# A transformer block with adaptive layer norm: w_mod regrouped by rows, late K columns, and another order for the start of the K projection

## The chip, the cores and the metric

The kernel runs on one core of a Trainium2 chip. The metric is the device time of one execution in microseconds (us). A time quoted for a kernel is the median of several executions; the profile is of one execution, and its span (first to last instruction) is about 1.8 us shorter than that execution's time.

## The reference

Two batches (B = 2) of 256 tokens, width D = 1152 (9 tiles of 128), two heads, everything in bf16:

```python
mod = (_silu(c) @ w_mod).reshape(B, 6, 1, D)
shift_a, scale_a, gate_a, shift_m, scale_m, gate_m = [mod[:, i] for i in range(6)]
h = _layernorm(x, axis=-1) * (1 + scale_a) + shift_a
qkv = (h @ wqkv).reshape(B, N, 3, H, Dh)
...                                  # attention, wo, second layer norm, fc1, gelu, fc2
return x + gate_m * m
```

Only the start matters here: before the first real matmul, the kernel needs x, its layer norm, `scale_a` (a product of silu(c) with 1152 columns of w_mod) and the K columns of wqkv.

## The kernel before

All work is written as units, which a small list scheduler puts on the engines. TensorE (PE) and the SP queue, which issues the loads, keep the order of the source text. `mm` is one matmul (line 692), `tr` one transpose (line 695), and every `dma` has line 673; so the profile shows these three lines for nearly everything, and shapes tell them apart.

The loads in order. The weights `WSC` for `scale_a` come in two halves, columns of tiles 0 to 3 and 4 to 8 (KC = 4), each in three pieces of three k-tiles:

```python
wmod_v = w_mod.rearrange("(k p) f -> p k f", p=P)
...
dma(CSB[0:18, :], c.rearrange("b (k p) -> (b k) p", p=P), 18 * 256, "ld_c", eng="act")
for b in range(2):
    dma(X[:, 2 * b:2 * b + 2, :], xv[b], ...)
for (ka, kb) in ((0, KC), (KC, KT)):
    for k0, k1 in ((0, 3), (3, 6), (6, 9)):
        dma(WSC[:, k0:k1, ka * P:kb * P], wmod_v[:, k0:k1, D + ka * P:D + kb * P], ...)
    for kt in range(ka, kb):
        dma(WK[:, kt, :], wqkv_v[:, kt, D:2 * D], ...)
for k0 in range(0, KT, 3):
    dma(WSH[:, k0:k0 + 3, :], wmod_v[:, k0:k0 + 3, 0:D], ...)        # shift_a
```

The start of PE's program. `warm` issues matmuls on zeros that are only there to keep PE's clock up. `sca(a, b)` adds k-tiles a to b into the scale columns of tiles 0 to 3 (2-column matmuls). `xn_T(t)` transposes the normalised token tile t. `hk(kt, b)` scales a transposed tile by `1 + scale_a` into `HK`, the moving operand of the K projection:

```python
xn_T(1)
warm(1, "c")
sca(0, 3)
xn_T(0)
warm(1, "d")
sca(3, 6)
warm(2, "e")
sca(6, 9)
hk(0, 0)
sc1a(0, KC)
hk(1, 0)
... # ScalarE: copies of the other tiles, hk(2, 0), hk(3, 0)
xn_T(3, 0, 8)
xn_T(2, 0, 8)
k_first(0)                       # first-half K, batch 0, k-tile 0
xn_T(3, 8, 9)
xn_T(2, 8, 9)
k_first(1)
... # k_first(2), k_first(3), batch 1, two pairs
for kt in range(KT):
    mod_kt(WSC, kt, 0, "scb_%d" % kt, (KC, KT))     # second-half scale columns
sc1a(KC, KT)
... # hk(4..8), second-half K
```

Behind the K projection come the rows of `shift_a` ("shift rows", 2-row matmuls), their transposes, the last K tile (column tile 8, `proj(WK, 8, 17, HK, 0)`), and then Q.

Of the kernel before, what the change touches and what calls it, by code (L numbers as in the profile page):

```python
# [500 lines left out]
P = 128  # L501
# [43 lines left out]
def build_kernel(nc, x, c, wqkv, wo, w_mod, w_fc1, w_fc2, out):  # L545
# [5 lines left out]
    with (  # L551
# [81 lines left out]
        CSB = sb(misc(256), 256)  # L633
# [32 lines left out]
        wmod_v = w_mod.rearrange("(k p) f -> p k f", p=P)  # L666
# [31 lines left out]
        dma(CSB[0:18, :], c.rearrange("b (k p) -> (b k) p", p=P), 18 * 256, "ld_c", eng="act")  # L698
        for b in range(2):
            dma(X[:, 2 * b:2 * b + 2, :], xv[b], 2 * P * D * 2, "ld_x%d" % b)  # L700
        for (ka, kb) in ((0, KC), (KC, KT)):
            w = (kb - ka) * P
            for k0, k1 in ((0, 3), (3, 6), (6, 9)):
                dma(WSC[:, k0:k1, ka * P:kb * P], wmod_v[:, k0:k1, D + ka * P:D + kb * P], (k1 - k0) * P * w * 2,
                    "ld_sc%d_%d" % (ka, k0), run=w * 2)
            for kt in range(ka, kb):
                dma(WK[:, kt, :], wqkv_v[:, kt, D:2 * D], P * D * 2, "ld_wk%d" % kt, run=2304)
        for k0 in range(0, KT, 3):
            dma(WSH[:, k0:k0 + 3, :], wmod_v[:, k0:k0 + 3, 0:D], 3 * P * D * 2, "ld_sh%d" % k0, run=2304)

# [13 lines left out]
        for i in range(5):  # L724
            S.unit("pe", 430.0, "warm_a%d" % i)
            mm(ps32(5), IDENT, Q4B, True, True)
        CT_PS = ps16(6, 0, 18)
        S.unit("pe", 100, "c_T")
        tr(CT_PS, CSB[0:18, :], IDENT[0:18, 0:18])
        act(200, lambda e: e.activation(out=TH, in_=CT_PS, func=ACTF.Tanh, scale=0.5), [CT_PS], [TH], "c_tanh")  # L730
        dve(170, lambda e: e.tensor_scalar(out=HC, in0=CT_PS, scalar1=0.5, scalar2=None, op0=ALU.mult), [CT_PS], [HC], "c_half")
# [37 lines left out]
        XB = [(4, 5, 3), (6, 5, 7)]  # L769
# [32 lines left out]
        def hk(kt, b, eng="dve"):  # L802
            dst = HK[:, kt, b * 256:(b + 1) * 256]
            s1 = ps32(7, 0, 1) if kt == 0 and b == 0 else SC1A[:, kt * 2 + b:kt * 2 + b + 1]
            src = xslot(b, kt) if kt < KC else HX[:, kt, b * 256:(b + 1) * 256]
            if eng == "act":
                act(c_act(256, 1), lambda e: e.activation(out=dst, in_=src, func=ACTF.Copy, scale=s1), [src, s1], [dst], "hk_%d_%d" % (kt, b))
                return
            dve(345 if kt < KC else 285, lambda e: e.tensor_scalar(out=dst, in0=src, scalar1=s1, scalar2=None, op0=ALU.mult),
                [src, s1], [dst], "hk_%d_%d" % (kt, b))  # L810
# [7 lines left out]
        KB = [(0, 1, 2, 3), (4, 5, 6)]  # L818
# [27 lines left out]
        warm(7, "b")  # L846
# [5 lines left out]
        xn_T(0)  # L852
        warm(1, "d")
        sca(3, 6)
        warm(2, "e")
        sca(6, 9)
        hk(0, 0)
        sc1a(0, KC)
        hk(1, 0)
        xn_T_copy(0, 4, 8, "act")  # L860
        xn_T_copy(0, 8, 9, "act")
        hk(2, 0, "act")
        hk(3, 0, "act")
        xn_T(3, 0, 8)
        xn_T(2, 0, 8)

        def k_first(kt):
            for i in range(4):
                k_pair((kt,), i, 0)

        k_first(0)
        xn_T(3, 8, 9)
        xn_T(2, 8, 9)
        k_first(1)
# [9 lines left out]
        for kt in range(KT):  # L884
            mod_kt(WSC, kt, 0, "scb_%d" % kt, (KC, KT))
        sc1a(KC, KT)
        for kt in range(KC, KT):
            for b in range(2):
                hk(kt, b)
        k_pair(range(KC), 2, 1)  # L890
        for kt in range(KT):
            dma(WQ[:, kt, :], wqkv_v[:, kt, 0:D], P * D * 2, "ld_wq%d" % kt, run=2304)
            dma(WSM[:, kt, :], wmod_v[:, kt, 4 * D:5 * D], P * D * 2, "ld_sm%d" % kt, run=2304)
# [11 lines left out]

        def proj(W, j, dst_j, H, bank):
# [7 lines left out]
        k_pair(range(5), 3, 1, bank=1)  # L914
        S.unit("pe", KT * c_mm(CH) + 100.0, "shr")
        for kt in range(KT):
            for j, (f0, f1) in enumerate(sh_split):
                mm(psum[32 * j:32 * j + 2, 1024:1024 + (f1 - f0) * 128], ST[:, kt:18:9], WSH[:, kt, f0 * 128:f1 * 128],
                   kt == 0, kt == KT - 1, tile_position=(0, 32 * j))
        copy_on("dve", SHR[0:98, :], psum[0:98, 1024:1024 + CH], CH, False, "shr_ev")  # L920
        k_pair(range(5, KT), 3, 1, bank=1)
        S.unit("pe", KT * 27.0, "shT")
        for j, (f0, f1) in enumerate(sh_split):
            for f in range(f0, f1):
                mm(ps32(2, f * 2, 2), SHR[0:98, (f - f0) * 128:(f - f0 + 1) * 128], IDENT[0:98, 32 * j:32 * j + 2], f == 0, f == KT - 1,
                   skip_group_check=True)
        dma(WV, wqkv_v[:, :, 2 * D:3 * D], D * D * 2, "ld_wv", run=2304)
        for k0 in range(0, KT, 3):
            dma(WMODR[:, k0:k0 + 3, :], wmod_v[:, k0:k0 + 3, 2 * D:4 * D], 3 * P * 2 * D * 2, "ld_modr%d" % k0)
        MT1 = ps32(2, 0, 18)  # L930
        dve(170, lambda e: e.tensor_copy(SHA, MT1), [MT1], [SHA], "sha")
        for kt in range(KT):
            for b in range(2):
# [5 lines left out]
                else:  # L939
                    dve(260, lambda e, src=src, dst=dst, s2=s2: e.tensor_scalar(out=dst, in0=src, scalar1=s2, scalar2=None, op0=ALU.add),  # L940
                        [src, s2], [dst], "hx_%d_%d" % (kt, b))
        proj(WK, 8, 17, HK, 0)
# [5 lines left out]
                    "xn_1", "bn_ln1_2_1", "xn_0", "bn_ln1_2_2", "aggr_ln1_2", "var_ln1_3", "veps_ln1_2", "xn_3", "xn_2", "hk_0_0", "sc1a_0", "hk_1_0",  # L948
                    "hk_0_1", "hk_1_1", "hk_2_1", "hk_3_1", "sc1a_4"] + ["hk_%d_%d" % (kt, b) for kt in range(KC, KT) for b in range(2)],
            "act": ["ld_c", "c_tanh", "sum_ln1_0", "sq_ln1_0", "sum_ln1_3", "sq_ln1_3", "xnT_cp0_4", "xnT_cp0_8", "hk_2_0", "hk_3_0",  # L950
# [317 lines left out]
        S.order_after(by["rstd_ln1_2"], by["rstd_ln1_3"])  # L1268
# [67 lines left out]
```

## Time and profile before

| | before |
|---|---|
| median of 3 runs | 245.66 us (245.56 to 245.70) |
| span of the profiled run | 243.9 us, granted clock given as 1.00 |
| PE busy | 98% |
| K begins / second-half K begins | 12.06 / 19.13 us |
| last matmul starts | 240.62 us |

From the page of the kernel before: busy time and share of the span by engine, with the number of instructions; then PE's busy tenths in 40 slices of the span, the DMA engines' busy tenths, and the chain by line. (`arena` is the kernel's one buffer in on-chip memory, `psum` the memory that PE writes its results to, SPq the issuing of loads by SP.)

```profile
PE 239.0 (98%) x1755; PEld 147.4 (60%) x1755; DVE 120.9 (50%) x218; ACT 66.5 (27%) x134; POOL 21.3 (9%) x39
...
PE   7999999999999999999999999999999999999994
...
DMA  6999999999995999979953498030000000000000
...
PE psum L692 90%; DMA arena<-in_w_mod_dram 5%; SPq L673 2%; PE psum L695 1%; DVE arena L1259 0%; DVE arena L1260 0%
```

PE is busy in all slices but the first and the last, and 90% of the chain are matmuls. The DMA engines are busy for nine tenths or more in all but two of the first 17 slices (104 us), but the chain names a DMA for 5% only. So the time is PE's work plus the head in which PE has no work yet.

The chain in order of time (start, length, what), before:

```profile
7.11 11.57 DMA arena<-in_w_mod_dram
18.68 0.05 issue
18.73 40.89 PE psum L692 x310
```

The last thing PE waits for is a piece of w_mod, up to 18.68 us; from there on PE runs on alone. The timeline of the head, before (start, length, engine, line, operation, out<-in, count, and in brackets the idle time before it and what ended it):

```profile
10.32 1.23 DVE L764 TENSOR_SCALAR arena<-arena 128x1152 bf16<-128x1152 bf16 x2 [0.58 <-POOL arena L755]
...
11.13 1.09 PE L695 MATMUL psum<-arena 128*128 128x128 bf16 x16
11.46 0.35 DVE L809 TENSOR_SCALAR arena<-psum 128x256 bf16<-128x256 bf16 x1
...
12.06 1.04 PE L692 MATMUL psum<-arena 128*128 128x256 bf16 x8
...
12.93 0.28 PE L695 MATMUL psum<-arena 128*128 128x128 bf16 x2
...
13.04 5.33 PE L692 MATMUL psum<-arena 128*128 128x256 bf16 x71
...
18.73 26.54 PE L692 MATMUL psum<-arena 128*128 128x2 bf16 x219 [0.35 <-DMA arena<-in_w_mod_dram]
```

VectorE (DVE) normalises tiles 3 and 2 until 11.55. PE transposes 16 tiles from 11.13, and the 128x256 matmuls of K begin at 12.06. The 71 matmuls from 13.04 are K and then 2-column scale columns; PE idles behind them, waiting for w_mod, until 18.73. (The bracket counts from the modelled end of the last matmul: 0.35 us. From the last issue at its own pace it is 0.49 us.) The waits of PE in the first 35 us (engine and line, what it waited for: us in total, times, longest):

```profile
PE psum L692 <- POOL arena L715: 1.5, 1, 1.5
PE psum L692 <- DMA arena<-in_w_mod_dram: 0.4, 1, 0.4
```

There is one wait on w_mod, of 0.4 us. The first line is the wait before PE's first instruction of all.

### The profile page before, as it was taken

Reading aid. Unit: us, or ns where it says so; the run is one execution under the profiler, and the core shown is the slowest. Engines: PE = TensorE matmul, PEld = TensorE weight load, DVE = VectorE, ACT = ScalarE, POOL = GpSimd, SP = SyncE. Lnnn points to the kernel's source line nnn. Section 1 sums busy time; section 2 is a strip of 40 time slices with the busy share of each in tenths; the row PEclk is TensorE's granted clock in tenths of the full one; section 3 lists DMA queues with packets and bytes.
Section 4 is the critical chain, followed back from the end, with each engine's and each line's share of the span. In section 5 each row is a group of like instructions: output and inputs, shape, how many; then the busy total and the mean of one; then the engine's idle time right before and its main releaser. Section 6 shows DMA issues by size and latency. Waiting matters only on the chain.

```text
span 243.9 us, 4070 instructions
## 1 busy us (share of the span) xinstructions
PE 239.0 (98%) x1755; PEld 147.4 (60%) x1755; DVE 120.9 (50%) x218; ACT 66.5 (27%) x134; POOL 21.3 (9%) x39
## 2 busy tenths in 40 slices
PE   7999999999999999999999999999999999999994
PEld 2698754556667666898444444444656565656584
DVE  3814398596997899689999500000022211111112
ACT  5730340345424206973233222223000000000000
POOL 1400000000021186400000000020000000000000
DMA  6999999999995999979953498030000000000000
GB/s 234 333 381 391 389 392 389 398 411 409 389 350 171 343 390 392 393 264 393 312 173 86 145 329 300 0 86 14 0 16 19 16 16 19 16 27 21 19 16 19
DMA packets 30140, 51.59 MB, mean 212 GB/s; under 512 B 1703, under 2 KB 15787, under 8 KB 30123
## 3 DMA queue, kind: packets, MB, share of 16 engines
q1 hardware_dynamic: 29680, 50.14, 57.5%
q0 software_dynamic: 416, 1.19, 1.6%
q8 instruction: 14, 0.23, 0.4%
q14 instruction: 3, 0.02, 0.0%
q10 hardware_dynamic: 27, 0.00, 0.0%
HBM read 50.14 MB, written 1.19 MB: 210 GB/s over the span
## 4 chain that ended last, share of the span: by engine, by line
PE 91%; DMA 5%; SPq 2%; issue 0%; DVE 0%
PE psum L692 90%; DMA arena<-in_w_mod_dram 5%; SPq L673 2%; PE psum L695 1%; DVE arena L1259 0%; DVE arena L1260 0%
## 5 line engine op out<-in xcount | busy, mean ns | idle before, releaser
L692 PE MATMUL psum<-arena 128*128 128x384 bf16 (+12 forms) x1666 | 235.8, 308 | 1.9 <-POOL arena L715 1.5
L692 PEld LDWEIGHTS psum<-arena 128*128 128x128 bf16 (+4 forms) x1666 | 142.2, 97 | 91.3 <-issue 4.7
L1054 DVE SCALAR_TENSOR_TENSOR arena<-arena 128x1152 f32<-128x1152 bf16 x32 | 44.7, 1413 | 0.6
L1259 DVE TENSOR_TENSOR arena<-psum,arena 128x384 f32<-128x384 f32 (+3 forms) x14 | 7.0, 500 | 68.0 <-PE psum L692 68.0
L1168 ACT ACTIVATE arena<-psum 128x512 bf16<-128x512 f32 (+1 forms) x44 | 22.4, 520 | 42.7 <-PE psum L692 42.7
L687 ACT ACTIVATE arena<-psum 128x512 bf16<-128x512 f32 (+6 forms) x35 | 19.0, 560 | 39.8 <-PE psum L692 39.1
L689 DVE CAST arena<-psum 128x512 bf16<-128x512 f32 (+3 forms) x14 | 8.9, 645 | 11.9 <-PE psum L692 11.9
L673 POOL DMA_DIRECT2D dit_scratch<-arena x3 | 1.8, 616 | 115.9 <-DVE arena L689 59.1
L1136 POOL TENSOR_TENSOR arena<-arena 128x384 f32<-128x384 f32 x12 | 10.9, 914 | 11.2 <-DVE arena L1135 9.6
L1081 DVE CAST arena<-psum 72x32 bf16<-72x32 f32 x1 | 0.2, 188 | 21.3 <-PE psum L692 21.3
L743 DVE BATCH_NORM_STATS2 arena<-arena 128x6 f32<-128x384 f32 (+1 forms) x18 | 9.5, 548 | 0.1
L1141 ACT ACTIVATE arena<-arena 128x1152 bf16<-128x1152 f32 x4 | 5.3, 1343 | 11.1 <-DVE arena L1140 11.1
L1135 DVE TENSOR_TENSOR arena<-psum,arena 128x384 f32<-128x384 f32 x12 | 6.5, 552 | 1.5 <-PE psum L692 1.4
L1260 DVE TENSOR_TENSOR arena<-arena 128x384 bf16<-128x384 f32 (+3 forms) x14 | 7.0, 501 | 0.5
L695 PE MATMUL psum<-arena 128*128 128x128 bf16 (+1 forms) x89 | 7.1, 219 | 0.0
L695 PEld LDWEIGHTS psum<-arena 128*128 128x128 bf16 (+1 forms) x89 | 5.8, 98 | 2.0 <-issue 0.8
L1158 ACT ACTIVATE arena<-psum,arena 128x128 bf16<-128x128 bf16 x16 | 6.0, 456 | 1.7 <-PE psum L695 1.1
L1155 DVE TENSOR_SCALAR arena<-psum,arena 128x128 bf16<-128x128 bf16 x20 | 5.4, 335 | 1.9 <-PE psum L695 1.9
L1061 DVE TENSOR_REDUCE arena<-arena 128x36 f32<-128x1152 f32 x4 | 5.4, 1346 | 0.0
L1058 DVE STREAM_TRANSPOSE arena<-arena 128x1152 f32<-128x1152 f32 x4 | 5.4, 1363 | 0.0
L984 ACT ACTIVATE arena<-psum,arena 128x256 bf16<-128x256 f32 x8 | 3.7, 472 | 1.3 <-PE psum L692 0.9
L980 DVE TENSOR_REDUCE arena<-psum 128x2 f32<-128x512 f32 x4 | 2.8, 689 | 1.8 <-PE psum L692 1.8
(47 smaller groups left out, 45.2 us busy)
## 6 DMA issues: line engine op xcount, KB each, us to landing
arena<-in_w_fc_dram SPq DMA_DIRECT2D x9, 1152.0 KB, 7.6
arena<-in_w_fc_dram SPq DMA_DIRECT2D x4, 2592.0 KB, 17.5
arena<-in_wqkv_dram SPq DMA_DIRECT2D x18, 288.0 KB, 10.2
arena<-in_w_mod_dram SPq DMA_DIRECT2D x3, 1728.0 KB, 20.2
arena<-in_w_mod_dram SPq DMA_DIRECT2D x3, 864.0 KB, 13.8
arena<-in_w_mod_dram SPq DMA_DIRECT2D x9, 288.0 KB, 10.5
arena<-in_wqkv_dram SPq DMA_DIRECT2D x1, 2592.0 KB, 16.6
arena<-in_wo_dram SPq DMA_DIRECT2D x1, 2592.0 KB, 24.4
```

Of the source, the lines that this page charges most:

```text
L673: return S.op(eng, 500.0 if eng == "sp" else 150.0, lambda e: e.dma_start(dst, src), reads=[src], writes=[dst], name=name, dma_bytes=nbyte ...
L687: act(c_act(n), lambda e: e.activation(out=dst, in_=src, func=ACTF.Copy), [src], [dst], name)
L689: dve(c_dve_psum16(n) if psum16 else c_dve_psum32(n), lambda e: e.tensor_copy(dst, src), [src], [dst], name)
L692: S.instr(lambda e: e.matmul(o, lhsT=l, rhs=r, start=st, stop=sp, **kw), reads=[l, r], writes=[o])
L695: S.instr(lambda e: e.transpose(o, i_, idn), reads=[i_, idn], writes=[o])
L743: dve(550, lambda e, s=s, o=o: e.bn_stats(out=o, in_=s), [s], [o], "bn_%s_%d" % (tag, ci))
L1054: dve(1270, lambda e, w=w, s=s, acc=acc: e.scalar_tensor_tensor(out=acc, in0=w, scalar=s, in1=acc, op0=ALU.mult, op1=ALU.add), [w, s, acc] ...
L1135: dve(550, lambda e, o=o, ga=ga, x1c=x1c: e.tensor_tensor(out=x1c, in0=o, in1=ga, op=ALU.mult), [o, ga], [x1c], "wo_t1_%d_%d" % (t, ci))
L1136: S.op("pool", 930, lambda e, xs=xs, x1c=x1c: e.tensor_tensor(out=x1c, in0=x1c, in1=xs, op=ALU.add), reads=[x1c, xs], writes=[x1c], name=" ...
L1168: act(c_act(ntok), lambda e: e.activation(out=dst, in_=o, func=ACTF.Gelu_apprx_tanh), [o], [dst], "gelu_%d_%d" % (f, tok0))
L1259: dve(c_dve_psum32(w), lambda e, o=o, gm=gm, t1=t1: e.tensor_tensor(out=t1, in0=o, in1=gm, op=ALU.mult), [o, gm], [t1], "fc2_t1_%d_%d" % ( ...
L1260: dve(c_dve_32(w), lambda e, t1=t1, x1c=x1c, ost=ost: e.tensor_tensor(out=ost, in0=t1, in1=x1c, op=ALU.add), [t1, x1c], [ost], "fc2_out_%d ...
```

## The change

Four things in one:

1. **Rows.** A partition gets 9 neighbouring rows of w_mod instead of rows 128 apart, so that c can be loaded as two whole rows. Its transposition into columns then takes nine small transposes instead of one.
2. **Late columns.** The last 128 of K's columns are left out of the loads of the first four K tiles and loaded in one go behind the shift rows' weights. 131 KB less stand ahead of the second-half w_mod pieces.
3. **K's start.** K begins behind tiles 0 and 2 instead of behind all four; tile 3 is transposed between K matmuls. Tile 0 moves behind the last scale columns, DVE's order follows, and other PSUM banks make room. A scaled tile of the second half (`hk(4, 0)`) reads its scale straight from PSUM.
4. **Shift stage.** The third K pair is finished before the shift rows, the last K tile is split around the shift transposes, and Q's weights are loaded two tiles ahead of each scale_m tile.

```diff
-        wmod_v = w_mod.rearrange("(k p) f -> p k f", p=P)
+        wmod_v = w_mod.rearrange("(p k) f -> p k f", p=P)
 ...
-        dma(CSB[0:18, :], c.rearrange("b (k p) -> (b k) p", p=P), 18 * 256, "ld_c", eng="act")
+        dma(CSB[0:2, :], c, 2 * D * 2, "ld_c", eng="act")
 ...
-                dma(WK[:, kt, :], wqkv_v[:, kt, D:2 * D], P * D * 2, "ld_wk%d" % kt, run=2304)
+                w = D if ka else D - P
+                dma(WK[:, kt, 0:w], wqkv_v[:, kt, D:D + w], P * w * 2, "ld_wk%d" % kt, run=2304)
 ...                                   (after the loads of WSH)
+        dma(WK[:, 0:KC, D - P:D], wqkv_v[:, 0:KC, 2 * D - P:2 * D], 2 * KC * P * P * 2, "ld_wk17", run=2304)
 ...
-        for i in range(5):                                            (warm_a)
+        for i in range(4):
-        tr(CT_PS, CSB[0:18, :], IDENT[0:18, 0:18])
+        for kt in range(KT):
+            tr(ps16(6, 2 * kt, 2), CSB[0:2, kt:D:KT], IDENT[0:2, 0:2])
 ...
-        warm(7, "b")
+        warm(8, "b")
 ...
         sca(0, 3)
-        xn_T(0)
         warm(1, "d")
         sca(3, 6)
-        warm(2, "e")
+        warm(1, "e")
         sca(6, 9)
+        xn_T(0)
+        xn_T(2, 0, 8)
         hk(0, 0)
 ...
-        xn_T(3, 0, 8)
-        xn_T(2, 0, 8)
-        k_first(0)
-        xn_T(3, 8, 9)
+        k_first(0, (0, 1, 3))
+        k_first(1, (0, 1, 3))
+        xn_T(3)
         xn_T(2, 8, 9)
-        k_first(1)
+        k_first(0, (2,))
+        k_first(1, (2,))
 ...                                   (banks, hk(KC, 0), WQ/WSM load order, shift stage, DVE and ACT orders)
```

More of the change, by code (lines that the diff above doesn't have):

```diff
@@ L632, in build_kernel @@
         ONES = sb(misc(256), 256)
-        CSB = sb(misc(256), 256)
+        CSB = sb(O_P, 2304)
         TH = sb(misc(72), 72, F32)
@@ L723, in build_kernel @@
         dve(270, lambda e: e.memset(Q4B, 0.0), [], [Q4B], "zq4b")
-        for i in range(5):
+        for i in range(4):
             S.unit("pe", 430.0, "warm_a%d" % i)
             mm(ps32(5), IDENT, Q4B, True, True)
-        CT_PS = ps16(6, 0, 18)
-        S.unit("pe", 100, "c_T")
-        tr(CT_PS, CSB[0:18, :], IDENT[0:18, 0:18])
-        act(200, lambda e: e.activation(out=TH, in_=CT_PS, func=ACTF.Tanh, scale=0.5), [CT_PS], [TH], "c_tanh")
-        dve(170, lambda e: e.tensor_scalar(out=HC, in0=CT_PS, scalar1=0.5, scalar2=None, op0=ALU.mult), [CT_PS], [HC], "c_half")
+        S.unit("pe", KT * 27.0, "c_T")
+        for kt in range(KT):
+            tr(ps16(6, 2 * kt, 2), CSB[0:2, kt:D:KT], IDENT[0:2, 0:2])
+        CT_PS = ps16(6, 0, 18).rearrange("p (k b) -> p b k", b=2)
+        th3, hc3 = (a.rearrange("p (b k) -> p b k", b=2) for a in (TH, HC))
+        act(200, lambda e: e.activation(out=th3, in_=CT_PS, func=ACTF.Tanh, scale=0.5), [CT_PS], [TH], "c_tanh")
+        dve(170, lambda e: e.tensor_scalar(out=hc3, in0=CT_PS, scalar1=0.5, scalar2=None, op0=ALU.mult), [CT_PS], [HC], "c_half")
         i3 = IDENT.rearrange("p (a i) -> p i a", a=4)
@@ L766, in build_kernel @@
                 [xt, m, rs], [xn], "xn_%d" % t)
-        XB = [(4, 5, 3), (6, 5, 7)]
+        XB = [(4, 5, 3), (6, 2, 7)]
         def xslot(b, kt, n=256):
@@ L803, in hk @@
             dst = HK[:, kt, b * 256:(b + 1) * 256]
-            s1 = ps32(7, 0, 1) if kt == 0 and b == 0 else SC1A[:, kt * 2 + b:kt * 2 + b + 1]
+            s1 = ps32(7, 2 * kt, 1) if kt in (0, KC) and b == 0 else SC1A[:, kt * 2 + b:kt * 2 + b + 1]
             src = xslot(b, kt) if kt < KC else HX[:, kt, b * 256:(b + 1) * 256]
@@ L816, in k_mm @@
                    kt == KT - 1, skip_group_check=True)
-        KB = [(0, 1, 2, 3), (4, 5, 6)]
+        KB = [(0, 1, 5, 3), (4, 2, 6)]
         ev_rr = [0]
@@ L859, in build_kernel, with k_first @@
         hk(1, 0)
+        xn_T_copy(0, 8, 9, "act")
         xn_T_copy(0, 4, 8, "act")
-        xn_T_copy(0, 8, 9, "act")
         hk(2, 0, "act")
         hk(3, 0, "act")
-        xn_T(3, 0, 8)
-        xn_T(2, 0, 8)
-        def k_first(kt):
-            for i in range(4):
+        def k_first(kt, pairs=range(4)):
+            for i in pairs:
                 k_pair((kt,), i, 0)
-        k_first(0)
-        xn_T(3, 8, 9)
+        k_first(0, (0, 1, 3))
+        k_first(1, (0, 1, 3))
+        xn_T(3)
         xn_T(2, 8, 9)
-        k_first(1)
+        k_first(0, (2,))
+        k_first(1, (2,))
         xn_T_copy(1, 4, 8, "act")
@@ L885, in build_kernel @@
             mod_kt(WSC, kt, 0, "scb_%d" % kt, (KC, KT))
+        hk(KC, 0)
         sc1a(KC, KT)
@@ L888, in build_kernel @@
             for b in range(2):
-                hk(kt, b)
+                if kt > KC or b:
+                    hk(kt, b)
         k_pair(range(KC), 2, 1)
-        for kt in range(KT):
-            dma(WQ[:, kt, :], wqkv_v[:, kt, 0:D], P * D * 2, "ld_wq%d" % kt, run=2304)
-            dma(WSM[:, kt, :], wmod_v[:, kt, 4 * D:5 * D], P * D * 2, "ld_sm%d" % kt, run=2304)
+        for i in range(KT):
+            for kt in range(2 * i, min(2 * i + 2, KT)):
+                dma(WQ[:, kt, :], wqkv_v[:, kt, 0:D], P * D * 2, "ld_wq%d" % kt, run=2304)
+            dma(WSM[:, i, :], wmod_v[:, i, 4 * D:5 * D], P * D * 2, "ld_sm%d" % i, run=2304)
         for kt in range(KC, KT - 2):
@@ L904, in qk_evac, with proj_part @@
             ev_rr[0] += 1
+        def proj_part(W, j, H, bank, ka, kb):
+            S.unit("pe", (kb - ka) * c_mm(512), "qk_17_%d" % ka)
+            for kt in range(ka, kb):
+                mm(ps32(bank), W[:, kt, j * 128:(j + 1) * 128], H[:, kt, :], kt == 0, kt == KT - 1)
         def proj(W, j, dst_j, H, bank):
@@ L913, in build_kernel @@
         SHR = sb(O_P, 768)
-        k_pair(range(5), 3, 1, bank=1)
-        S.unit("pe", KT * c_mm(CH) + 100.0, "shr")
-        for kt in range(KT):
-            for j, (f0, f1) in enumerate(sh_split):
-                mm(psum[32 * j:32 * j + 2, 1024:1024 + (f1 - f0) * 128], ST[:, kt:18:9], WSH[:, kt, f0 * 128:f1 * 128],
-                   kt == 0, kt == KT - 1, tile_position=(0, 32 * j))
-        copy_on("dve", SHR[0:98, :], psum[0:98, 1024:1024 + CH], CH, False, "shr_ev")
-        k_pair(range(5, KT), 3, 1, bank=1)
+        k_pair(range(KT), 3, 1, bank=1)
+        for k0 in range(0, KT, 3):
+            S.unit("pe", 3 * c_mm(CH) + 50.0, "shr_%d" % k0)
+            for kt in range(k0, k0 + 3):
+                for j, (f0, f1) in enumerate(sh_split):
+                    mm(psum[32 * j:32 * j + 2, 0:(f1 - f0) * 128], ST[:, kt:18:9], WSH[:, kt, f0 * 128:f1 * 128],
+                       kt == 0, kt == KT - 1, tile_position=(0, 32 * j))
+        copy_on("dve", SHR[0:98, :], psum[0:98, 0:CH], CH, False, "shr_ev")
+        proj_part(WK, 8, HK, 7, 0, 4)
         S.unit("pe", KT * 27.0, "shT")
@@ L924, in build_kernel @@
             for f in range(f0, f1):
-                mm(ps32(2, f * 2, 2), SHR[0:98, (f - f0) * 128:(f - f0 + 1) * 128], IDENT[0:98, 32 * j:32 * j + 2], f == 0, f == KT - 1,
+                mm(ps32(0, f * 2, 2), SHR[0:98, (f - f0) * 128:(f - f0 + 1) * 128], IDENT[0:98, 32 * j:32 * j + 2], f == 0, f == KT - 1,
                    skip_group_check=True)
+        proj_part(WK, 8, HK, 7, 4, KT)
+        qk_evac(17, 7)
         dma(WV, wqkv_v[:, :, 2 * D:3 * D], D * D * 2, "ld_wv", run=2304)
@@ L929, in build_kernel @@
             dma(WMODR[:, k0:k0 + 3, :], wmod_v[:, k0:k0 + 3, 2 * D:4 * D], 3 * P * 2 * D * 2, "ld_modr%d" % k0)
-        MT1 = ps32(2, 0, 18)
+        MT1 = ps32(0, 0, 18)
         dve(170, lambda e: e.tensor_copy(SHA, MT1), [MT1], [SHA], "sha")
@@ L941, in build_kernel @@
                         [src, s2], [dst], "hx_%d_%d" % (kt, b))
-        proj(WK, 8, 17, HK, 0)
         dma(WO, wo_v, D * D * 2, "ld_wo", run=2304)
@@ L947, in build_kernel @@
             "dve": ["zq4b", "c_half", "c_silu", "bn_ln1_1_0", "bn_ln1_1_1", "bn_ln1_1_2", "aggr_ln1_1", "veps_ln1_1", "bn_ln1_2_0",
-                    "xn_1", "bn_ln1_2_1", "xn_0", "bn_ln1_2_2", "aggr_ln1_2", "var_ln1_3", "veps_ln1_2", "xn_3", "xn_2", "hk_0_0", "sc1a_0", "hk_1_0",
-                    "hk_0_1", "hk_1_1", "hk_2_1", "hk_3_1", "sc1a_4"] + ["hk_%d_%d" % (kt, b) for kt in range(KC, KT) for b in range(2)],
-            "act": ["ld_c", "c_tanh", "sum_ln1_0", "sq_ln1_0", "sum_ln1_3", "sq_ln1_3", "xnT_cp0_4", "xnT_cp0_8", "hk_2_0", "hk_3_0",
+                    "xn_1", "bn_ln1_2_1", "bn_ln1_2_2", "aggr_ln1_2", "veps_ln1_2", "xn_0", "var_ln1_3", "xn_2", "hk_0_0", "sc1a_0", "hk_1_0",
+                    "xn_3", "hk_0_1", "hk_1_1", "hk_2_1", "hk_3_1", "hk_%d_0" % KC, "sc1a_4", "hk_%d_1" % KC] + ["hk_%d_%d" % (kt, b) for kt in range(KC + 1, KT) for b in range(2)],
+            "act": ["ld_c", "c_tanh", "sum_ln1_0", "sq_ln1_0", "sum_ln1_3", "sq_ln1_3", "xnT_cp0_8", "xnT_cp0_4", "hk_2_0", "hk_3_0",
                     "xnT_cp1_4", "xnT_cp1_8"],
@@ L1267, in build_kernel @@
         S.order_after(by["gm_1_0"], by["gm_0_8"])
-        S.order_after(by["rstd_ln1_2"], by["rstd_ln1_3"])
+        S.order_after(by["rstd_ln1_3"], by["rstd_ln1_2"])
         for u in S.units:
```

## The prediction

> **What bounds the kernel now.** TensorE. The page gives PE 98% busy over a 243.9 us span; the chain that ended last is 90% matmuls. In the timeline, matmuls keep their own pace from 18.73 us to the end (109 ns for 128x256, 216 ns for 128x512, 27 ns for 2 columns), but for 0.1 to 0.2 us at a few changes of shape. That work stays, so only the head can win.
>
> The head (timeline, landings of DMAs):
> - Warm-up matmuls take 427 ns until about 7.2 us, then 216 ns. The first w_mod pieces land at 7.7, 9.1, 10.3, the first K tile at 11.1.
> - K begins at 12.06, behind 16 transposes of LN1 tiles 3 and 2.
> - 48 K matmuls and scale columns run gapless to 18.21. Then PE waits 0.49 us for the last second-half w_mod piece (18.68), late on one DMA engine: its first share landed at 16.43, and a 16 KB instruction packet of 1.1 us started at 15.4.
> - Shift rows run 28.83 to 30.39; their last piece lands at 29.19.
>
> **What the change does.**
> 1. K begins after the transposes of tiles 0 and 2 alone. But tile 3's nine (0.5 us) move between K matmuls, so PE's work before the second-half scale columns is not reduced. My step count: scale columns end at 10.7, tile 0 transposes 11.2, first scaled tile on DVE 11.4 to 11.8 (0.35 us), K at 11.85. Then 48 x 109 + 10 x 56 ns = 5.8 us: second-half scale columns begin at 17.6 to 17.9, against 17.41. The early start is given back.
> 2. Four K tiles lose 128 columns: 4 x 32 KB less ahead of the second-half w_mod pieces, 0.33 us at these stages' 390 GB/s. The last piece should land near 18.35, and PE hardly waits. Scale columns end at 18.85 to 19.05 instead of 19.13.
> 3. The 131 KB come back as 512 packets of 256 B. "DMA: Bandwidth & Descriptors" (Why small descriptors are slow) says that small packets carry a fixed overhead; the trace agrees for larger ones (46 ns for 1 KB, 95 for 2304 B). Estimate 0.5 us instead of 0.33; landing near 29.5, needed at 30.9.
> 4. Two Q tiles per scale_m tile: the last Q lands near 39.5 instead of 42.0, but was needed only near 44: no gain.
> 5. w_mod by 9 rows: same packet sizes, neutral. c needs nine transposes at the cold clock (estimate 0.5 us instead of 0.12); one warm-up less (0.43 us) pays.
> 6. The split last K tile leaves 5 x 216 ns = 1.08 us instead of 1.94 to cover shift copy and first HX tiles (0.2 + 0.6 us): barely enough.
>
> **Sum.** Gain 0.1 to 0.5 us, from the w_mod wait. Predicted 245.4 us (before 245.66), 8 in 10: 244.8 to 245.9. Faster by over 2%: 1%; within 2%: 98%; slower: 1%.
>
> **What would show it.** K begins at 11.6 to 12.0; second-half scale columns begin after 17.5 with a wait under 0.2 us; second-half K begins about 0.25 us earlier; the later matmul stream is shifted by that and otherwise the same; no new wait before Q.
>
> **What would make it wrong.** The w_mod row order changes the DMA rate (first pieces not at 10.3 us); the clock warms at another moment ("TensorE: Matmul & The Clock Gate", What's actually happening: a free-running window); HX not ready when the split tile ends, some tenths; the instruction packet on another piece; later scale_m loads upsetting VectorE's order.

## The result, and the profile after

| | before | after |
|---|---|---|
| median, with range | 245.61 us (245.37 to 245.70, 4 runs) | 245.51 us (244.99 to 245.72, 4 runs) |
| ratio, 95% interval | | 0.9994 (0.9977 to 1.0012) |
| span of the profiled run | 243.9 us | 243.7 us |
| K begins / second-half K begins | 12.06 / 19.13 us | 12.29 / 19.32 us |
| last matmul starts | 240.62 us | 240.85 us |

A ratio is the mean time of one kernel's fast runs over that of the other's fast runs of the same rounds, so it is not quite the ratio of the medians. The total was predicted: no change that can be told from noise. But the profile of after does not show the predicted gain. Its matmul stream ends 0.23 us *later*, and the span is shorter only because less time passes behind the last matmul. So both parts needed an explanation, and that the median lies 0.10 us lower is no support for the predicted gain of 0.1 to 0.5 us.

From the page of the kernel after:

```profile
PE 237.9 (98%) x1752; PEld 147.4 (60%) x1762; DVE 121.0 (50%) x218; ACT 66.5 (27%) x134; POOL 21.5 (9%) x39
...
PE   7899999999999999999999999999999999999995
...
DMA  6999999999995999989942498003000000000100
...
PE psum L692 92%; DMA arena<-in_w_mod_dram 3%; PE psum L695 2%; SPq L673 1%; DVE arena L1274 0%; DVE arena L1275 0%
```

The chain in order of time, after:

```profile
3.38 7.42 DMA arena<-in_w_mod_dram
10.80 0.05 issue
10.85 0.47 PE psum L692 x12
11.31 0.97 PE psum L695 x17
12.28 0.01 issue
12.29 1.48 PE psum L692 x12
```

The last DMA on the chain now ends at 10.80 us instead of 18.68: it is the third *first-half* piece of w_mod. From there on it is PE alone. The timeline of the head, after:

```profile
9.80 0.71 PE L692 MATMUL psum<-arena 128*128 128x2 bf16 x13 [0.69 <-DMA arena<-in_w_mod_dram]
...
10.18 0.58 DVE L768 TENSOR_SCALAR arena<-arena 128x1152 bf16<-128x1152 bf16 x1 [0.37 <-POOL arena L751]
...
10.85 0.47 PE L692 MATMUL psum<-arena 128*128 128x2 bf16 x12 [0.34 <-DMA arena<-in_w_mod_dram]
...
11.18 1.11 PE L695 MATMUL psum<-arena 128*128 128x128 bf16 x17
...
11.88 0.35 DVE L813 TENSOR_SCALAR arena<-psum 128x256 bf16<-128x256 bf16 x1 [1.12 <-PE psum L695]
...
12.29 1.48 PE L692 MATMUL psum<-arena 128*128 128x256 bf16 x12
...
13.61 0.72 PE L695 MATMUL psum<-arena 128*128 128x128 bf16 x10
...
14.17 17.39 PE L692 MATMUL psum<-arena 128*128 128x256 bf16 x214
```

PE waits before the scale columns at 9.80 and again before those at 10.85. Then come 17 transposes. DVE was idle for 1.12 us before its first scaled tile at 11.88, because the transposes of tile 0 now stand behind the last scale columns. K follows at 12.29, and ten transposes stand between its matmuls at 13.61. In the matmuls from 14.17 the view shows no wait at all. (That line goes on over K, scale columns and more K.) PE's waits in the first 35 us, after:

```profile
PE psum L692 <- POOL arena L717: 1.5, 1, 1.5
PE psum L692 <- DMA arena<-in_w_mod_dram: 1.0, 2, 0.7
PE psum L692 <- issue: 0.2, 1, 0.2
```

Where before there was one wait of 0.4 us on w_mod, there are now two, 1.0 us in all. The wait behind the first-half K is gone, and waits ahead of K have come up. (The 0.2 us of the last line are a pause at 31.56, behind the shift rows.)

### The profile page after: what moved, and what is told of

It reads as the page before. It is cut to its first block, busy times and chain, and to the rows that moved or that the text cites. A ratio compares the mean times of both kernels' runs of the same rounds, so it can differ in the third digit from the quotient of the medians.

```text
span 243.7 us, 4075 instructions
## 1 busy us (share of the span) xinstructions
PE 237.9 (98%) x1752; PEld 147.4 (60%) x1762; DVE 121.0 (50%) x218; ACT 66.5 (27%) x134; POOL 21.5 (9%) x39
## 3 DMA queue, kind: packets, MB, share of 16 engines
q0 software_dynamic: 416, 1.19, 1.8%
HBM read 50.14 MB, written 1.19 MB: 211 GB/s over the span
## 4 chain that ended last, share of the span: by engine, by line
PE 94%; DMA 3%; SPq 1%; issue 0%; DVE 0%
PE psum L692 92%; DMA arena<-in_w_mod_dram 3%; PE psum L695 2%; SPq L673 1%; DVE arena L1274 0%; DVE arena L1275 0%
## 5 line engine op out<-in xcount | busy, mean ns | idle before, releaser
L692 PE MATMUL psum<-arena 128*128 128x384 bf16 (+10 forms) x1655 | 234.0, 307 | 3.1 <-POOL arena L717 1.5
L692 PEld LDWEIGHTS psum<-arena 128*128 128x128 bf16 (+2 forms) x1665 | 141.6, 97 | 91.5 <-issue 3.9
L695 PEld LDWEIGHTS psum<-arena 128*128 128x128 bf16 (+1 forms) x97 | 6.3, 103 | 2.1 <-DMA arena<-in_c_dram 0.8
L751 POOL TENSOR_TENSOR arena<-arena 128x1 f32<-128x1 f32 x6 | 3.6, 596 | 2.3 <-DVE arena L750 2.3
## 6 DMA issues: line engine op xcount, KB each, us to landing
arena<-in_w_fc_dram SPq DMA_DIRECT2D x4, 2592.0 KB, 17.4
```

Source lines behind the costliest of these rows:

```text
L692: S.instr(lambda e: e.matmul(o, lhsT=l, rhs=r, start=st, stop=sp, **kw), reads=[l, r], writes=[o])
L695: S.instr(lambda e: e.transpose(o, i_, idn), reads=[i_, idn], writes=[o])
```

## The experiments

Because the effects are of a few tenths of a microsecond, and single executions differ by as much, every run's profile is read at the same landmarks. In the table, "piece 3" is the landing of the third first-half w_mod piece (the last of the 16 increments of its semaphore), "last piece" that of the third second-half piece, "columns" the start of the second-half scale columns. All are us from the span's start. The first six rows have K's old order, the others the new one. The three sets ran on different chips; each is compared with runs of the kernel before in its own rounds.

| run | piece 3 | K begins | K minus piece 3 | columns | last piece | second-half K | last matmul | span |
|---|---|---|---|---|---|---|---|---|
| before | 10.32 | 12.06 | 1.74 | 17.41 | 18.68 | 19.13 | 240.62 | 243.9 |
| before_again | 10.53 | 12.28 | 1.75 | 17.63 | 19.18 | 19.63 | 241.12 | 244.0 |
| rows_alone | 10.97 | 12.24 | 1.27 | 17.59 | 18.59 | 19.05 | 240.54 | 243.9 |
| before_more_instr | 11.02 | 12.29 | 1.27 | 17.64 | 18.28 | 19.08 | 240.86 | 243.8 |
| cols_alone | 10.83 | 12.10 | 1.27 | 17.45 | 17.83 | 18.67 | 240.40 | 243.6 |
| cols_again | 10.84 | 12.26 | 1.42 | 17.61 | 18.15 | 18.84 | 240.56 | 243.6 |
| after | 10.80 | 12.29 | 1.49 | 18.10 | 17.52 | 19.32 | 240.85 | 243.7 |
| after_again | 10.81 | 12.30 | 1.49 | 18.11 | 17.50 | 19.33 | 240.86 | 243.7 |
| after_oldrows_newc | 11.13 | 12.62 | 1.49 | 18.43 | 17.82 | 19.66 | 241.18 | 244.1 |
| after_nowarm | 11.13 | 12.62 | 1.49 | 18.43 | 17.88 | 19.66 | 241.18 | 244.1 |
| after_fullcols | 10.10 | 11.59 | 1.49 | 17.40 | 17.99 | 18.62 | 240.15 | 243.2 |
| after_t0fill | 11.16 | 12.21 | 1.05 | 18.02 | 17.84 | 19.24 | 240.77 | 243.7 |
| after_oldrows (clock halved) | 10.96 | 12.74 | 1.78 | 19.74 | 17.69 | 20.97 | 242.49 | 245.6 |
| after_lesswarm (clock halved) | 10.78 | 12.71 | 1.93 | 19.55 | 17.53 | 20.77 | 242.30 | 245.2 |

### First set: did the row order delay the first pieces?

In the profile of after, piece 3 landed 0.48 us later than before, and one DMA engine was late: the last share of the second piece landed at 9.75, the second last at 8.60. Theory R blamed w_mod's new row order, theory C the two-row load of c, theory N chance. All four kernels were timed in five rounds.

**after_again**: the changed kernel, no edit.

> The changed kernel unaltered, a second look. Theory R (the 9-row order of w_mod makes one DMA engine late): again the last share of the 2nd and 3rd w_mod piece lands 0.4 us or more behind the second last, at 9.5 to 9.9 and 10.6 to 11.0 us, K begins at 12.2 to 12.4. Theory C (the c load as 2 packets makes it late): the same here. Theory N (lateness of one engine is chance, in any run of either kernel): the pieces land as often as not at 9.1 and 10.3, K begins at 11.8 to 11.9. Time all theories: ratio 0.998 to 1.001.

Measured: piece 3 at 10.81 and K at 12.30, as R and C expected, but the second piece at 8.98 with no late share, which they did not. Median 245.58 us (244.96 to 247.52, 6 runs) against 245.49 us (245.18 to 246.18, 11 runs), ratio 1.0021 (0.9989 to 1.0054). The runs at 247.47 and 247.52 have a mean clock of 0.993, the others of 0.999 or 1.000. That was new, and is taken up below.

**after_oldrows_newc**: the old row order, with c in two rows.

```diff
-        wmod_v = w_mod.rearrange("(p k) f -> p k f", p=P)
+        wmod_v = w_mod.rearrange("(k p) f -> p k f", p=P)
-            tr(ps16(6, 2 * kt, 2), CSB[0:2, kt:D:KT], IDENT[0:2, 0:2])
+            tr(ps16(6, 2 * kt, 2), CSB[0:2, kt * P:(kt + 1) * P], IDENT[0:2, 0:2])
```

> The changed kernel with w_mod in the old row order, c still loaded as 2 rows with nine transposes (of contiguous columns). Theory R: no late share, 3rd w_mod piece at 10.2 to 10.4 us, K begins at 11.8 to 11.9, second-half K 0.3 to 0.5 us earlier than in the changed kernel (18.8 to 19.0), time ratio to before about 0.998. Theory C: still late, piece 3 at 10.6 to 11.0, K at 12.2 to 12.4. Theory N: either.

Measured: piece 3 at 11.13, later than in the changed kernel. R falls: the old row order does not bring the early landing back. Ratio 1.0015 (0.9991 to 1.0040); one run of six at 247.50 with clock 0.993.

**after_oldrows**: the old row order, the old load of c, one transpose, five `warm_a`.

```diff
-        dma(CSB[0:2, :], c, 2 * D * 2, "ld_c", eng="act")
+        dma(CSB[0:18, :], c.rearrange("b (k p) -> (b k) p", p=P), 18 * 256, "ld_c", eng="act")
 ...   (and the rows, the transpose and warm_a as before)
```

> The changed kernel with the old row order and the old c load (18 rows of 256 B, one transpose, five warm-ups). Theories R and C: no late share, 3rd w_mod piece at 10.2 to 10.4 us, K begins at 11.7 to 11.9. Theory N: either. Time ratio to before about 0.998 by R and C.

Measured: piece 3 at 10.96. As the whole explanation, C falls too. The profiled run happened to be one with the halved clock (247.34 us, the one of six). Ratio 1.0003 (0.9983 to 1.0024).

**rows_alone**: the kernel before with only the rows and c changed (nine transposes, four `warm_a`).

> The kernel before with only the row order of w_mod and the c load changed (nine transposes, one warm-up less). Theories R and C: 3rd w_mod piece lands at 10.6 to 11.0 instead of 10.3 us with one share late, K begins 0.3 to 0.5 us later than before (12.4 to 12.6), and as PE then waits less for the last second-half piece, the end is 0 to 0.4 us later: ratio 1.000 to 1.002. Theory N: lands at 10.3 as often as not.

Measured: piece 3 at 10.97, but K at 12.24, not the 12.4 to 12.6 that was expected, and second-half K at 19.05. Ratio 0.9997 (0.9982 to 1.0012). Over all 14 profiles piece 3 lands between 10.10 and 11.16 us. The six looks with both old rows and old c give 10.32, 10.53, 10.83, 10.84, 10.96 and 11.02, and the seven with both new 10.10 to 11.16, so the row order is not what decides it. Theory N stands for most of the spread.

A part of C is not excluded. In five of the eight profiles with c in two rows (rows_alone, after, after_oldrows_newc, after_nowarm, after_t0fill), SP needs 1.10 to 1.19 us to issue the first w_mod piece, and 0.43 us in the other three and in all six with the old load. From the chains of before and after (start, length, what):

```profile
1.71 0.43 SPq L673
...
1.70 1.10 SPq L673
```

In these five, piece 3 lands at 10.80 to 11.16, in the other nine at 10.10 to 11.02. Why only some executions have the long issue was not tested.

The table shows more than the set asked for. In the new order K begins 1.49 us after piece 3 in five profiles out of five with the full clock and the change's own PE order. In the old order it takes 1.27 us in three of the four profiles in which piece 3 lands after 10.8 (1.42 in the fourth, cols_again, in which PE was still busy with warm-ups until 11.06). When piece 3 is early, K begins at 12.06 or 12.28 all the same, since DVE normalises tiles 3 and 2 until 11.55 or 11.77 and PE has to transpose them. So behind a late piece 3 the new order, meant to start K earlier, starts it 0.22 us later; with an early one it does start it earlier, at 11.59 in after_fullcols.

### Second set: the tail, the clock, and where tile 0 belongs

**before_again**: the kernel before, one look.

> The kernel before unaltered, a second look at its head and its tail. If the late engine is chance in every run of either kernel, the third w_mod piece lands anywhere from 10.3 to 11.1 us here too, and K begins at 12.06 to 12.3 all the same. The tail theory (the output's landing waits for a 16 KB instruction packet that falls at the end): the last instruction packet starts within 0.2 us of the last matmul and ends 1.2 us or more after it, the output before the last lands 2.3 to 2.5 us after the last matmul, the span ends 3.2 to 3.4 us after it. Rival (chance): 2.8 to 3.0 as in the changed kernel.

Measured: piece 3 at 10.53. The wait behind the first-half K is larger this time: the last w_mod piece lands at 19.18, second-half K begins at 19.63. The tail is *not* as expected: the last 16 KB instruction packet (each profile has 14 of them on a DMA queue of the kind "instruction") ended 0.82 us after the last matmul's start, the output before the last landed at 1.87, and the span ended 2.90 us behind it, as in the changed kernel. In the first profile these were 1.33, 2.38 and 3.29. So the tail differs between two executions of one kernel. PE's waits in the first 35 us in this second look:

```profile
PE psum L692 <- POOL arena L715: 1.5, 1, 1.5
PE psum L692 <- DMA arena<-in_w_mod_dram: 0.6, 1, 0.6
PE psum L692 <- DVE arena L744: 0.2, 1, 0.2
```

**before_more_instr**: eight tiny extra matmuls in the wait for the last piece.

```diff
             mod_kt(WSC, kt, 0, "scb_%d" % kt, (KC, KT))
+            if kt == 5:
+                S.unit("pe", 8 * 27.0, "extra")
+                for i in range(8):
+                    mm(ps32(7, 64 + 2 * i, 2), WSC[:, 0, 0:128], ST[:, 0:18:9], True, True)
```

> The kernel before with 8 tiny extra matmuls (16 instructions on PE, as many as the change adds with its nine transposes) put into the 0.49 us in which PE waits for the last second-half w_mod piece. Tail theory (the number of PE instructions decides where the last 16 KB instruction packet falls): that packet starts 0.3 us or more before the last matmul, the span ends 2.8 to 2.95 us after the last matmul instead of 3.3, the second-half K begins as before (19.0 to 19.15), ratio about 0.998. Rival (the tail is set by something else in the change, or chance): 3.2 to 3.4, ratio 1.000.

Its result is wrong (relative error 0.69), which was not intended. The extra matmuls carry the start flag and lie in the bank in which the scale columns are being summed. The Trainium skill, "PSUM — Partial Sum Buffer" (Terms, zero region), says that such a matmul clears the written bits of the whole 2 KiB bank, so that sums under way are overwritten; the wrong result agrees. Its times are read with that reserve. The tail came out as expected (packet from 0.27 us before to 0.81 us after the start of the last matmul, span end at 2.91), but before_again has nearly the same packet end and span end without any edit, so these prove nothing for the number of instructions. The ratio was 1.0027 (1.0009 to 1.0046) instead of 0.998: slower, in part by one run of six at 247.42 with clock 0.992. The stretch from second-half K to the first attention matmul took 28.30 us instead of 28.01; the rest was not followed up.

The *start* of the packet does go with the number of instructions. Over all 14 profiles, with 1755 weight loads counted on PE (six profiles, both looks at before among them) the last packet starts between 0.13 us before and 0.46 us after the start of the last matmul; with 1759 (after_nowarm) 0.19 us before it; with 1762 to 1764 (seven profiles, after and before_more_instr among them) 0.27 to 0.44 us before it. But this packet's own length varies from 0.95 to 1.48 us, and 0.95 against 1.28 is what sets before_again's tail apart from that of the first profile of before, more than the earlier start.

The other part of the tail theory holds in all 14 profiles: the output before the last lands 1.05 to 1.26 us after the end of the last 16 KB instruction packet, and these packets take 0.88 to 1.53 us. The tail came out between 2.88 and 3.32 us long: the number of instructions moves the packet's start, and the packet's length, which varies by itself, moves it as much again.

**after_nowarm**: without the single warm-ups "c", "d" and "e".

```diff
-        warm(1, "c")
-        warm(1, "d")
-        warm(1, "e")
```

> The changed kernel without the three single warm-up matmuls between the scale-column groups: 0.65 us more idle PE between 8.4 and 11.2 us. Clock theory (idle PE in one free-running window of 3.4 us halves the clock in the next, which costs 2 us): at least 3 of the 6 runs at 247 us or more, with a mean clock of 0.993, and median ratio of the runs up to 1.004. Rival (the runs at 247.5 us have nothing to do with idle PE): at most 1 of 6, as in the changed kernel, where it was 2 of 10.

Measured: one run of six with a halved clock (247.06, clock 0.993); ratio 1.0007 (0.9986 to 1.0027). The expectation of at least three was missed. Either the theory was wrong or 0.65 us of PE work was too small a dose.

**after_t0fill**: tile 0's transposes ahead of the last scale columns, two more warm-ups in PE's waits.

```diff
-        warm(1, "d")
+        warm(3, "d")
 ...
-        sca(6, 9)
         xn_T(0)
+        sca(6, 9)
         xn_T(2, 0, 8)
```

> The changed kernel with the transposes of LN1 tile 0 ahead of the last three scale-column groups and two more warm-up matmuls, both in time in which PE waits for w_mod. If K's start is bound by these transposes standing behind the last w_mod piece, K begins 0.4 to 0.5 us earlier (11.8 to 11.9), second-half K at 18.85 to 18.95 instead of 19.3, everything behind it shifted alike; no run at 247 us in the clock theory; tail as in the changed kernel. Ratio to before 0.997 to 0.998. Rival (K's start is bound by DVE or the first K tile): K begins at 12.2 to 12.3, ratio 1.000.

Measured: K begins 1.05 us after piece 3 instead of 1.49, so 0.44 us is won behind the landing, as expected. But piece 3 landed at 11.16 in this run, and K at 12.21, so the clock times that were expected (11.8 to 11.9) did not come. The view shows no wait of PE on w_mod in its first 35 us:

```profile
PE psum L692 <- POOL arena L717: 1.5, 1, 1.5
```

Median 245.43 us (245.29 to 246.03, 5 runs) against 245.81 us, ratio 0.9992 (0.9980 to 1.0004); no run with a halved clock. It is not clear of the kernel before.

### Third set: the late columns, the new order, and more of the clock

**cols_alone** and **cols_again**: the kernel before with the late columns only; the same kernel twice.

```diff
-                dma(WK[:, kt, :], wqkv_v[:, kt, D:2 * D], P * D * 2, "ld_wk%d" % kt, run=2304)
+                w = D if ka else D - P
+                dma(WK[:, kt, 0:w], wqkv_v[:, kt, D:D + w], P * w * 2, "ld_wk%d" % kt, run=2304)
 ...
+        dma(WK[:, 0:KC, D - P:D], wqkv_v[:, 0:KC, 2 * D - P:2 * D], ...)
```

> The kernel before with the late K columns only (128 columns of four K tiles loaded behind the shift rows), nothing else. My theory now: the late columns are the part of the change that pays, and the new order of K's start gives it back. Then K begins as before (1.27 us after the third w_mod piece or at 12.06, whichever is later), the last second-half piece lands in full by 17.4 to 17.9 instead of 18.3 to 19.2, second-half K begins at 18.5 to 18.8 (before: 19.05 to 19.63), the end 0.4 to 0.6 us earlier: ratio 0.9975 to 0.999. Rival (the late columns gain nothing, or wait behind their 256 B packets): second-half K at 19.05 or later, or a new wait before Q; ratio 1.000.

> The same kernel a second time, for the interval and a second profile: the same numbers.

Measured: the last piece lands at 17.83 and 18.15 instead of 18.28 to 19.18, and second-half K begins at 18.67 and 18.84 instead of 19.05 to 19.63. That is the direction expected, but in the second both are beyond the expected ranges (17.4 to 17.9, 18.5 to 18.8). Of this, 0.23 us is lost again: from second-half K to the first attention matmul it takes 28.24 us in both looks, 28.01 in both looks at before. The timeline of cols_alone shows where (PEld is PE's weight load):

```profile
19.22 0.17 DVE L801 COPY arena<-psum 128x10 f32<-128x10 f32 x1 [5.79 <-PE psum L692]
19.43 1.07 DVE L811 TENSOR_SCALAR arena<-arena 128x256 bf16<-128x256 bf16 x5
19.77 0.66 PEld L692 LDWEIGHTS psum<-arena 128*128 128x128 bf16 x7 [0.34 <-DVE arena L811]
```

The weights of the next matmul are held up for 0.34 us by DVE's line 811, the first scaled tile of the second half, which itself stands behind the copy of the scale columns at 19.22. The change itself has a remedy for that place: it scales that tile straight from PSUM, ahead of the copy, and in its profile the stretch takes 28.04 us. The times say less than the profiles: ratios 0.9992 (0.9959 to 1.0024) and 0.9986 (0.9956 to 1.0016). The kernel before had a run at 247.94 with clock 0.992 among its eleven, which favours every kernel of this set. Without that run the two means, 245.57 and 245.48, stand against 245.58, with a standard deviation of 0.2 to 0.3 us between runs. So the expected 0.4 to 0.6 us of the total did not show in the times.

**after_fullcols**: the changed kernel with whole K tiles.

```diff
-                w = D if ka else D - P
-                dma(WK[:, kt, 0:w], wqkv_v[:, kt, D:D + w], P * w * 2, ...)
+                dma(WK[:, kt, :], wqkv_v[:, kt, D:2 * D], P * D * 2, ...)
-        dma(WK[:, 0:KC, D - P:D], ...)
```

> The changed kernel with the four K tiles loaded whole again, everything else of the change kept. My theory (the new order of K's start costs): K begins 1.49 us after the third w_mod piece lands, second-half scale columns begin at 18.0 to 18.4, the last second-half piece lands at 18.0 to 19.2, second-half K at 19.3 to 19.8, ratio 1.000 to 1.002. Rival (the order gains): second-half K at 19.05 or earlier, ratio under 0.999.

Measured: piece 3 landed at 10.10, the earliest of all, and with it K (11.59), the columns (17.40) and second-half K (18.62) came earlier than either theory's numbers. The rule of 1.49 us holds again (11.59 - 10.10). This run therefore does not weigh the two theories by its second-half K. It also shows that with whole K tiles the last piece can land at 17.99, earlier than in cols_again, so that the late columns move that landing by less than the four old-order profiles with whole tiles suggest. Ratio 0.9985 (0.9954 to 1.0015), mean 245.45 against 245.58 without the run at 247.94.

**after_lesswarm**: as after_nowarm, and without the four warm-ups behind `veps` and `rstd`.

```diff
-        for n, behind in ((1, "bn_ln1_1_1"), (1, "aggr_ln1_1"), (2, "veps_ln1_1"), (2, "rstd_ln1_1")):
+        for n, behind in ((1, "bn_ln1_1_1"), (1, "aggr_ln1_1")):
```

> The changed kernel without the three single warm-ups and without the four warm-ups behind veps and rstd: 1.5 us less PE work between 7.2 and 11.2 us. Clock theory (the clock halves for one 3.4 us window behind a window with too little PE work, and the phase of the windows is chance): more runs with a mean clock under 0.996 and a time of 247 us or more than the changed kernel's 2 of 10: at least 3 of 6. Rival: at most 1 of 6.

Measured: four of six runs with a mean clock of 0.993, at 246.32, 246.53, 247.02 and 247.60 us; the other two at 245.29 and 245.48. As it stands, with clock *and* 247 us asked for, the expectation was missed (two of six, where the rival allowed one); by the clock alone it is met (four of six). The profiled run is one of the four. Its windows (start and end, length, then busy us and instructions of PE, PEld, DVE, ACT and POOL, then PE's granted clock, DMA share and GB/s), cut at the borders of the trace's clock records, whose lengths are multiples of 3.41 us:

```profile
4.59:8.00 3.41, 3.41 (x9) 1.14 (x8) 3.21 (x9) 3.38 (x6) 1.50 (x4) 1.00 0.89 270
8.00:11.41 3.41, 2.13 (x51) 1.86 (x51) 2.31 (x7) 1.29 (x3) 1.98 (x4) 1.00 1.01 345
11.41:14.83 3.42, 3.42 (x26) 2.81 (x24) 1.27 (x4) 2.03 (x4) 0.00 (x0) 0.50 1.06 385
14.83:18.24 3.41, 3.41 (x39) 3.11 (x37) 1.13 (x4) 1.30 (x2) 0.00 (x0) 1.00 1.07 379
```

The 1.00 of the first line is no record: this trace has none before 8.00, and the matmuls there still take 427 ns. (The first profile of before has no clock record at all, so its clock of 1.00 says nothing of its head either.) In the window from 8.00 PE was busy for 2.13 of 3.41 us, with 51 mostly tiny matmuls; in the next, its clock was 0.50, just as K began. The same view of after_oldrows, whose profiled run also had it:

```profile
8.36:11.78 3.42, 2.19 (x50) 1.71 (x49) 2.01 (x6) 1.24 (x2) 1.73 (x3) 1.00 1.01 351
11.78:15.19 3.41, 3.41 (x24) 2.73 (x22) 1.27 (x4) 2.02 (x4) 0.00 (x0) 0.50 1.06 381
```

And of the changed kernel and of before_again, whose profiled runs had not:

```profile
9.21:12.62 3.41, 2.48 (x45) 1.98 (x46) 1.88 (x8) 0.94 (x4) 1.46 (x2) 1.00 1.04 385
12.62:16.03 3.41, 3.41 (x39) 3.10 (x37) 1.69 (x6) 2.58 (x5) 0.00 (x0) 1.00 1.07 374
```

```profile
8.30:11.71 3.41, 3.27 (x62) 2.36 (x59) 2.59 (x9) 2.58 (x5) 1.77 (x3) 1.00 1.01 347
11.71:15.13 3.42, 3.39 (x38) 3.02 (x37) 1.86 (x8) 2.03 (x4) 0.00 (x0) 1.00 1.05 385
```

PE was busy for 2.13 and 2.19 us in the windows that were followed by half the clock, for 2.48 us in the changed kernel's and 3.27 us in before_again's at the same place, which were not. In the same view, the least busy head windows of the other profiles that kept the clock have 2.62 (after_nowarm), 2.81 (after_oldrows_newc), 2.95 (rows_alone), 3.01 (cols_alone), 3.05 (after_fullcols), 3.33 (after_again), 3.34 (after_t0fill) and 3.36 us (cols_again).

Busy time alone does not decide, however. In after_t0fill, the window that holds the program's last matmuls is busy for 2.18 us, less than the 2.19 us above, and the clock record of 1.00 goes on through it and the next window:

```profile
238.78:242.19 3.41, 2.18 (x63) 2.06 (x60) 1.38 (x6) 0.00 (x0) 0.00 (x0) 1.00 0.13 29
```

What does separate them is the number of columns of the moving operands that the matmuls of a window stream, counted from the shapes in the traces (an estimate, as some matmul records can be missing). The two head windows before a drop have 1.9 and 2.1 thousand columns, this one has 4.4 thousand, and the changed kernel's of 2.48 us has 3.5 thousand. In the 12 traces that have clock records, every window with up to 2.1 thousand columns was followed by half the clock (14 windows, 12 of them at the end of the program) and every one with 3.5 thousand or more was not (823). That the chip counts columns is not shown by this; that a 2-column matmul keeps the clock up less than its busy time suggests is.

The Trainium skill, "TensorE: Matmul & The Clock Gate" (What's actually happening), describes free-running windows of 3413 ns whose activity sets the clock; the records agree in length, and in that their phase differs from run to run (they begin at 8.00, 4.95, 5.79 and 4.89 us in these four profiles).

## Why the prediction was right, and where its steps were not

The time lay where it was predicted: 245.51 us against 245.4, no change of 2%. Point by point:

- **"Only the head can win": held.** From the start of second-half K to the first attention matmul it takes 28.01 us before and 28.04 after. No work of that stretch was removed.
- **"The early start is given back": held, and more than given back.** Nine transposes of tile 3 went between the K matmuls: from K's begin to the second-half scale columns it takes 5.35 us before and 5.81 after. The step that failed is its size at the other end, "K at 11.85" and "K begins at 11.6 to 12.0"; it was 12.29. The sum counted from piece 3 at 10.3, as in the one profile at hand. That landing is a draw between 10.1 and 11.2, and at 10.80 the same sum gives about 12.3, so the chain from the landing to K was counted rightly (about 1.5 us, measured 1.49) and the landing taken as fixed. Nor did the prediction notice that the old order needs only 1.27 us behind a late landing. In the new order, PE first transposes tile 0, only then can DVE scale it, and K waits for DVE. In the old order, tile 0 was transposed earlier, and DVE worked beside the 16 transposes. The test that moved only tile 0 (and two warm-ups) made it 1.05.
- **"PE hardly waits for the last second-half piece": held.** It landed at 17.52, sooner than the predicted 18.35, and PE began its scale columns at 18.10. The prediction kept the late DMA engine of the first profile, with the instruction packet at 15.4. In after, this packet started at 16.37. That this made the difference is not shown: in before_again it started at 16.97, and the piece landed at 19.18.
- **"Second-half K begins about 0.25 us earlier": failed.** It began 0.19 us later than in the first profile of before, and 0.31 us earlier than in the second. The gain was to come from the wait of 0.49 us. The experiments show that wait exchanged, not won: with the full clock the new order takes 0.22 us more up to K and 0.46 us more within it, 0.68 us, and in return loses a wait that was 0.49 us in one look, 0.77 us in the other (19.23 minus 18.46, at PE's own pace) and 0.24 us in rows_alone. It also makes the start depend on the third first-half piece instead of the last second-half one.
- **"c's nine transposes pay for one warm-up", "131 KB in 0.5 us", "last Q near 39.5", "1.08 us is enough": held.** The nine took 0.63 us instead of 0.12; the late columns landed 0.53 us after the last shift piece, in packets of 18 ns; the last Q tile landed at 38.98; no wait of PE on a load or another engine appeared before Q. rows_alone has the ratio 0.9997.
- **Not foreseen: the shorter span with the longer matmul stream.** The span ends 3.29 us after the last matmul's start in the first profile of before and 2.88 in after. The last instruction packet ended 1.33 us after that start in the one and 0.71 us in the other. Of this difference, 0.33 us are its earlier start, which goes with the change's seven more weight loads, and 0.30 its shorter length. The length varies without any edit: before_again has 0.95 us instead of 1.28, and a tail of 2.90.
- **Not foreseen: the clock.** The prediction named the clock's phase as a risk, but for the warm-up. The risk is that tile 0's transposes no longer fill PE's waits and a warm-up is gone, so that a window can fall under what keeps the clock up. The changed kernel had a halved clock in 2 of 10 runs, 2 us longer each; the kernel before in 1 of 38. That too little PE work in a window of the head causes such drops is well supported by after_lesswarm (four of six, against four of 28 in the kernels with the change's order and all its warm-ups) and by the windows above. That the *change* makes them more frequent is likely, as its head can leave less PE work in a window (2.48 us and 3.5 thousand columns in its first profile, but 3.33 us in its second; at the least 2.95 us in rows_alone, and 4.0 thousand columns in cols_alone), but the counts are too small to show it.

What stays open: whether the change is a few hundredths of a per cent faster in runs with the full clock (eight such runs have the mean 245.42, the 15 runs of before beside them 245.58, with a spread of about 0.3 in each), and whether the late columns together with the old order of K's start and the scaled tile straight from PSUM would be the best of all. The runs point there (second-half K at 18.67 and 18.84, with 0.23 us of DVE wait left), but that version was not run, and none of those that were is clear of the kernel before.

## What to carry to other kernels

When a head is bound by loads, count from each landing to the first useful matmul, and write down the chain of engines between them: moving a transpose behind the last-arriving piece put DVE into that chain and cost 0.22 us whenever that piece was late, though it looked like an earlier start. Look at a second profile of the *unchanged* kernel before explaining tenths of a microsecond: its landings, its longest wait and its tail moved by 0.2 to 0.5 us on their own. Put work that PE must do anyway into its waits, not behind them: besides the time itself, it can keep the clock up when the real work begins. In these traces, the columns that PE streamed in a window told the drops of the clock apart; its busy time did not.

## What the Trainium skill lacked or had wrong

- "TensorE: Matmul & The Clock Gate" (What's actually happening) has the clock fall back after an idle window of about 3.4 us. Here it fell behind windows that were not idle: PE was busy for 2.13 and 2.19 of 3.41 us, mostly with tiny matmuls, and the longest single pause in the window of after_oldrows was 1.06 us. The page's later section on a second failure mode speaks of short pauses, but neither gives an amount of work that keeps the clock up nor says how tiny matmuls count. In this case's traces it fell behind windows with up to 2.1 thousand streamed columns and held behind those with 3.5 thousand or more, while busy times of 2.18 us (held) and 2.19 us (fell) do not tell them apart.
- "Runtime: NRT & Kernel Launch" (Instruction fetch mechanics) does not say what the packets that fetch the program's own instructions do to stores: here 14 packets of 16 KB per run, 0.88 to 1.53 us each. The output before the last landed 1.05 to 1.26 us after the end of the last of them in all 14 profiles.
- "DMA: Bandwidth & Descriptors" gives an overhead per packet (Why small descriptors are slow) and one packet time, for its smallest transfer (Measured), but none for larger packets. Here a packet took 18 ns at 256 B, 46 ns at 1 KB and 95 ns at 2304 B.
